# Pooled attention into a soft mixture of experts: carrying three row groups of the last expert, cutting fewer weights and tiles into halves, and moving the slot sums

## The chip, the cores and the metric

The kernel runs on one core of one Trainium2 chip. The metric is the device time of one execution in microseconds (us). The core has five engines that run their own instruction lists: PE (matrix products; its weight loads are shown apart as PEld), DVE and ACT (elementwise work), POOL (which here issues all loads but one) and SP (which issues the first load and all stores). Sixteen DMA engines move the data.

## The reference, cut to what matters

```python
# attention: q, k, v are (8, 8, 576, 64); keys and values are averaged over 8 tokens
k_p = k.reshape(B, H, Sp, 8, D).mean(axis=3)
v_p = v.reshape(B, H, Sp, 8, D).mean(axis=3)
attn = softmax(scale * q @ k_p.T)
x = (attn @ v_p) as (4608, 512)
# soft mixture: 8 experts, 4 slots each
logits = x @ phi                                  # (4608, 32)
d = softmax of logits over the 4608 tokens        # dispatch
slot_input = (d.T @ x).reshape(8, 4, 512)
h = maximum(slot_input[e] @ w1[e], 0)             # (4, 1024)
slot_out[e] = h @ w2[e]                           # (4, 512)
c = softmax of logits over the 32 slots           # combine
return c @ slot_out                               # (4608, 512) float32
```

w1 and w2 are 16.8 MB each in float32, the output is 9.4 MB.

## The kernel before, in words

**Attention and dispatch (up to about 124 us).** The batch is worked in four pairs. For each pair PE averages keys and values (`pool_stage`), turns keys and queries, makes scores (`score_unit`), and `u_tile` makes the attention's output next to its logits in `xsa`. `weigh` (L333) sums the logits over the heads on PE and takes the exponential on ACT into `ee`; `gather` (L341) multiplies `ee` with x on PE and collects the slot inputs; `turn` writes the transposed exponentials into `cT` (32 slots, repeated over four row groups of partitions, by tokens), with their sums over tokens in `C`. For the last pair this is written out in L475 to L513: tokens tiles 0 to 3, then 4 to 6, then 7 and 8.

**First layer (L525 to L545).** `hidden(i)` makes the hidden values of four experts at a time, four products beside one another in four column groups of the array; `turn_hidden(i)` turns them into `hT`. `recC` is the reciprocal of the dispatch sums.

**Second layer (L549).** `second_layer(e, j0, j1, half)` adds the row groups j0 to j1 (of eight, FJ) of `w2[e]` to `so_ps`, a PSUM tile with the slots' outputs; four row groups run beside one another on four column groups of the array. Weights come by DMA with a cast to bf16: experts 0 to 3 into `big`, 4 and 5 into `qTa`, the first three row groups of expert 6 into `xsa` (L473), all 512 columns wide. The last five row groups of expert 6 and all of expert 7 come in halves of 256 columns, first the left halves, then the right ones, each in the pieces of `PIECES` (L92, L498 to L506). All of these are issued by POOL in the order of the text.

**The order at the end.** From L516 on, the order on PE, ACT, DVE and SP is the order of the text: each engine takes its instructions as they are written, and waits where an operand isn't ready. POOL's order is that of the text throughout. The written-out list is L656 to L685. `busy(n)` (L581) is a float32 product into a tile that nobody reads, a filler for PE. `row_sums` (L405) sums the exponentials over the slots for all tokens, ten matmuls with one-hot weights that read `cT` with a step of half the rows of a store group; `turn_sums` (L414) turns and inverts them into `recR`.

**Carrying.** The output of a tile of 128 tokens is `c @ slot_out`. For the first CARRY = 4 tiles the last row group of expert 7 (J7 = FJ - 1) does not pass through the slots' sum: `hz` holds that group's hidden values times `recC` (L568), `zT` is `hz` times the tokens' exponentials (L571 to L575), and `product(n, cols, True)` adds `zT` times the weights (L615) to the tokens times `so_a` (L616), which is the slots' sum without that group, scaled by `recC` on ACT (L632). So `so_a` can be made before the last piece of weights is there. All other tiles use `so`, the scaled sum of everything (L639, L618).

**Output.** Tokens are split in store groups of 4, 4, 2, 4, 8 and 14 rows per partition, 128 tokens a row, 36 tiles in all (GROUPS, L57). `put` (L625) scales a tile by `recR` on ACT or DVE in turn; `store` (L607) is a DMA on SP. The first SPLIT = 10 tiles are made and stored by halves of the columns, two tiles a DMA; the rest with whole rows, a group a DMA.

```python
begin(half):  so_a <- so_ps (ACT);  products 0, 1 (carried);  second_layer(7, J7, FJ, half)
              products 2, 3 (carried);  put 0 (ACT), put 1 (DVE), store 0-1
              so <- so_ps (ACT);  put 2 (DVE), put 3 (ACT), store 2-3
```

Of the kernel before, what the change touches and what calls it, by code (L numbers as in the profile page):

```python
# [18 lines left out]
def kernel(  # L19
# [37 lines left out]
    for rows in (4, 4, 2, 4, 8, 14):  # L57
        GROUPS.append((rows, base))
        base += 128 * rows
# [81 lines left out]
    for _ in range(95):  # L141
        nc.tensor.matmul(out=first[0:32, 0:16], lhsT=zeros[:, 0:32], rhs=zeros[:, 0:16], start=True, stop=True)
# [6 lines left out]
    onehot = consts.tile([128, 2 * MAXC - 1], BF)  # L149
# [39 lines left out]
    hz = consts.tile([128, 128], BF)  # L189
    for i in range(4):  # L190
        nc.gpsimd.memset(hz[:, 32 * i:32 * i + 32], 0.0)
# [213 lines left out]
    def row_sums():  # L405

        ps = ps_m.tile([NC, 4, 128], FP, name="R_ps", tag="m")
        for c, (_, t) in enumerate(quads + rest):
            nc.tensor.matmul(out=ps[:, 0:2 * t.shape[1]].rearrange("p (s r) i -> p s r i", r=2),   # L409
                             lhsT=onehot[:, MAXC - 1 - c:MAXC - 1 - c + NC], rhs=t,  # L410
                             start=(c == 0), stop=(c == NC - 1), skip_group_check=True)
        nc.scalar.copy(out=sums, in_=ps)
# [60 lines left out]
    load_w2(xsa[:, 0:1], E - 2, 1, 0, CUT6)  # L473
# [16 lines left out]
    def half_home(e, half):  # L490
        if e == E - 1:
            flat = xsa[:, 1, half * FJ * HC:(half + 1) * FJ * HC]
        else:
            c0 = CUT6 * DM + half * (FJ - CUT6) * HC
            flat = xsa[:, 0, c0:c0 + (FJ - CUT6) * HC]
        return flat.rearrange("p (j c) -> p j c", c=HC)

    w2_half = {}  # L498
    for half, cols in enumerate(halves):
        for e, j0, j1 in PIECES:  # L500
            home = half_home(e, half)
            i = 0 if e == E - 1 else CUT6
            nc.gpsimd.dma_start(out=home[:, j0 - i:j1 - i],  # L503
                                in_=moe_w2[e].rearrange("(p j) d -> p j d", j=FJ)[:, j0:j1, cols])
            for j in range(j0, j1):
                w2_half[e, j, half] = home[:, j - i]  # L506
# [42 lines left out]
    def second_layer(e, j0=0, j1=FJ, half=None):  # L549
        cols = slice(0, DM) if half is None else halves[half]  # L550
        for fj in range(j0, j1):
            g = fj % NG
            nc.tensor.matmul(out=so_ps[g * NS:(g + 1) * NS, cols], lhsT=hT[:, e, fj],  # L553
                             rhs=w2_at[e, fj] if half is None else w2_half[e, fj, half],
# [5 lines left out]
    turn_hidden(1)  # L560
    nc.vector.reduce_sum(out=recC, in_=C, axis=AX.X)
# [4 lines left out]
    J7 = FJ - 1  # L566
    P7 = (E - 1) % NG * NS
    nc.vector.tensor_scalar(out=hz[P7:P7 + NS], in0=h_sb[(E - 1) // NG][P7:P7 + NS, J7:F:FJ], scalar1=recC[P7:P7 + NS],  # L568
                            scalar2=None, op0=ALU.mult)
# [13 lines left out]

    def tiny(count, n=128):
        for _ in range(count):
            nc.tensor.matmul(out=idle[:, 0:n], lhsT=cT[:, 0, 0:128], rhs=cT[:, 0, 0:n], start=True, stop=True)
# [13 lines left out]
    n = 0  # L600
# [10 lines left out]
    def product(n, cols, carried=False):  # L611
        ps = ps_f.tile([128, DM], FP, name="f_ps", tag="f")[:, 0:cols.stop - cols.start]
        if carried:
            half = halves.index(cols)
            nc.tensor.matmul(out=ps, lhsT=zT[:, n], rhs=w2_half[E - 1, J7, half], start=True, stop=False)  # L615
            nc.tensor.matmul(out=ps, lhsT=tokens(n), rhs=so_a[:, cols], start=False, stop=True)  # L616
        else:
            nc.tensor.matmul(out=ps, lhsT=tokens(n), rhs=so[:, cols], start=True, stop=True)  # L618
# [97 lines left out]
```

## Time and profile before

| what | value |
|---|---|
| median of three runs | 175.86 us (175.48 to 176.15) |
| profiled execution, its own time | 176.28 us |
| its span | 174.5 us |
| PE, DVE, ACT, POOL busy | 134.5, 92.8, 89.7, 18.6 us |
| moved by DMA, read from and written to HBM | 61.93 and 9.44 MB |
| first store issued, last store issued | 148.07, 162.5 us |

The span is what the profile covers; the execution's time is 1.78 us longer. A line of the timeline reads: start, time from first start to last end of the merged instructions, engine, line of the kernel, operation, output <- inputs, shapes, count, and in brackets how long the engine was idle before and what ended it. PEq, SPq and the like are an engine's instruction queue. A line of the view by stretches reads: the stretch in us, its length, busy time with the count of instructions for PE, PEld, DVE, ACT and POOL, the granted clock of PE (1.00 is full), the share of the 16 DMA engines, and GB/s. A line of DMA issues reads: output <- input, queue, operation, count, size, and us from issue to landing. Bytes are counted at the destination, so a load that casts from float32 to bf16 counts half of what it reads.

### The profile page before, as it was taken

What the parts mean: (1) busy time and instruction counts of PE and PEld (TensorE: products, weight loads), DVE (VectorE), ACT (ScalarE), POOL (GpSimd) and SP (SyncE); (2) the same over time, 40 slices, a digit from 0 to 9 for tenths busy, and PEclk for the clock granted to TensorE, in tenths of its full rate; (3) what the DMA queues carried; (4) which work ended last, traced back from release to release, by engine and by line L of the source; (5) the groups of instructions that cost most, each with busy time, mean ns of one, the idle gap of its engine ahead of it and who ended that gap; (6) DMA issues with size and microseconds to landing.
All of it is one profiled execution on the core that took longest, in us unless ns stands there. A gap on an engine that the chain in (4) does not pass through costs nothing.

```text
span 174.5 us, 3115 instructions
## 1 busy us (share of the span) xinstructions
PE 134.5 (77%) x1236; PEld 74.1 (42%) x1236; DVE 92.8 (53%) x255; ACT 89.7 (51%) x174; POOL 18.6 (11%) x38
## 2 busy tenths in 40 slices
PE   5005778999899999999999899477878999898000
PEld 5002253565455655556555445343443234443000
DVE  5403263478879568796688735831650001699200
ACT  3201338977787838969379854454021103899000
POOL 7100111022101040000010002206010020000000
PEclk9999999999999999999999858955899999999855
DMA  5999999999999999999999999999999999899994
GB/s 195 246 215 218 217 220 207 224 213 217 212 216 221 215 209 224 213 215 216 218 214 212 214 225 218 212 212 214 222 218 216 195 195 166 289 358 438 451 421 210
DMA packets 10558, 41.14 MB, mean 236 GB/s; under 512 B 673, under 2 KB 6561, under 8 KB 6833
## 3 DMA queue, kind: packets, MB, share of 16 engines
q0 software_dynamic: 7248, 30.48, 86.1%
q1 hardware_dynamic: 3296, 10.49, 15.4%
q8 instruction: 9, 0.15, 0.3%
q14 instruction: 5, 0.03, 0.0%
HBM read 61.93 MB, written 9.44 MB: 409 GB/s over the span
## 4 chain that ended last, share of the span: by engine, by line
PE 55%; ACT 19%; DVE 8%; DMA 7%; issue 3%; POOL 1%; DVEq 0%; ACTq 0%; POOLq 0%
PE pool_ps L232 10%; ACT exa L306 8%; PE G_ps L344 7%; DMA phi_f<-in_moe_phi_dram 7%; PE sc L304 6%; PE u_ps L319 5%; PE q_ps L264 5%; DVE w_sb L592 4%; PE idle_ps L582 3%; PE lg_ps L337 3%; PE so_ps L553 3%; PE R_ps L409 3%; ACT vmeans L238 2%; PE h_ps L532 2%; PE turn_ps L248 2%
## 5 line engine op out<-in xcount | busy, mean ns | idle before, releaser
L306 ACT ACTIVATE exa<-sc 72x576 bf16<-72x576 f32 x64 | 39.4, 652 | 5.0 <-PE sc L304 4.3
L330 DVE TENSOR_TENSOR xsa<-u_ps,rec 128x384 bf16<-128x384 f32 x66 | 35.8, 553 | 1.2
L319 PE MATMUL u_ps<-vp,exa 72*128 72x97 bf16 (+1 forms) x304 | 25.9, 214 | 2.2 <-DVE xsa L330 1.3
L319 PEld LDWEIGHTS <-exa 72*128 72x128 bf16 (+1 forms) x320 | 18.4, 103 | 14.5 <-issue 4.1
L304 PE MATMUL sc<-qTa,kp 64*72 64x288 bf16 x128 | 21.8, 307 | 1.8 <-ACT exa L306 1.3
L232 PE MATMUL pool_ps<-big,pmat 128*128 128x512 bf16 x64 | 18.6, 411 | 0.7 <-ACT qTa L268 0.6
L324 DVE RECIPROCAL rec<-u_ps 128x4 f32<-128x4 f32 x69 | 10.9, 172 | 12.9 <-PE u_ps L319 12.7
L344 PE MATMUL G_ps<-xsa,ee 128*128 128x512 bf16 x36 | 12.8, 504 | 1.7 <-ACT ee L338 1.7
L264 PE MATMUL q_ps<-ident,big 128*128 128x128 bf16 x144 | 11.6, 219 | 0.8 <-DVE qTa L270 0.3
L304 PEld LDWEIGHTS <-kp 64*72 64x72 bf16 x128 | 8.0, 108 | 8.2 <-issue 2.9
L618 PE MATMUL f_ps<-so,cT 128*128 128x512 bf16 (+1 forms) x38 | 9.8, 344 | 1.0 <-ACT w_sb L590 0.8
L240 DVE TENSOR_REDUCE rsum<-rest_ps 128x64 f32<-128x512 f32 x8 | 5.5, 691 | 9.3 <-PE rest_ps L236 9.1
L264 PEld LDWEIGHTS <-big 128*128 128x128 bf16 x144 | 8.7, 97 | 2.9 <-issue 1.2
L268 ACT COPY qTa<-q_ps 128x768 bf16<-128x768 bf16 x8 | 6.3, 794 | 7.0 <-PE q_ps L264 7.0
L592 DVE TENSOR_SCALAR w_sb<-f_ps,recR 128x512 f32<-128x512 f32 (+1 forms) x15 | 9.6, 706 | 0.5 <-PE f_ps L618 0.5
L270 DVE COPY qTa<-q_ps 128x768 bf16<-128x768 bf16 x16 | 8.7, 552 | 1.7 <-PE q_ps L264 1.6
L183 PE MATMUL phi_ps<-spread,sel 128*128 128x256 bf16 x4 | 1.3, 396 | 10.5 <-DVE spread L178 10.5
L590 ACT ACTIVATE w_sb<-f_ps,recR 128x512 f32<-128x512 f32 (+1 forms) x15 | 8.7, 660 | 0.5 <-PE f_ps L618 0.3
L503 POOL DMA_DIRECT2D xsa<-in_moe_w_dram x8 | 6.0, 748 | 26.8 <-DMA qTa<-in_moe_w_dram 9.6
L232 PEld LDWEIGHTS <-pmat 128*128 128x128 bf16 x64 | 5.8, 103 | 6.5 <-issue 2.1
L592 DVE TENSOR_SCALAR exa<-f_ps,recR 128x256 f32<-128x256 f32 x8 | 3.7, 481 | 8.8 <-PE f_ps L616 8.6
L337 PE MATMUL lg_ps<-xsa,ident 128*128 128x288 bf16 (+3 forms) x48 | 7.8, 286 | 0.3 <-ACT xsa L328 0.3
(107 smaller groups left out, 166.4 us busy)
## 6 DMA issues: line engine op xcount, KB each, us to landing
w_sb<-in_moe_w_dram POOLq DMA_DIRECT2D x2, 3072.0 KB, 37.4
big<-in_q_dram POOLq DMA_DIRECT2D x4, 1152.0 KB, 12.4
big<-in_v_dram POOLq DMA_DIRECT2D x4, 1152.0 KB, 16.1
big<-in_moe_w_dram POOLq DMA_DIRECT2D x1, 4096.0 KB, 40.2
out_dram<-w_sb SPq DMA_DIRECT2D x1, 3584.0 KB, 10.6
big<-in_k_dram POOLq DMA_DIRECT2D x3, 1152.0 KB, 22.0
w_sb<-in_moe_w_dram POOLq DMA_DIRECT2D x2, 1024.0 KB, 18.6
qTa<-in_moe_w_dram POOLq DMA_DIRECT2D x1, 2048.0 KB, 31.0
```

The source lines that it names most:

```text
L232: nc.tensor.matmul(out=ps, lhsT=pmat, rhs=src[:, t:full * POOL:POOL, :], start=(t == 0), stop=(t == POOL - 1))
L264: nc.tensor.transpose(out=ps[:, t].rearrange("p n i -> p (n i)"), in_=q_sb[pair][:, tt:tt + 2, :].rearrange("p t d -> p (t d)"), identity= ...
L270: nc.vector.tensor_copy(out=dst, in_=ps)
L304: nc.tensor.matmul(out=ps[:, r, 0:S // 2], lhsT=kp[pair][rows, n], rhs=qT[pair][rows, n].rearrange("p t i -> p (t i)"), start=True, stop=True)
L306: nc.scalar.activation(out=dst.rearrange("p r (i t) -> p r i t", t=NU), in_=ps[:, :, 0:S // 2].rearrange("p r (t i) -> p r i t", i=NI), fu ...
L319: nc.tensor.matmul(out=ps[rows, hh], lhsT=ex[b][:, hh].rearrange("p r t -> p (r t)")[:, c:c + rows.stop - rows.start], rhs=vp[(2 * pair + ...
L324: nc.vector.reciprocal(out=rec, in_=ps[:, :, XW])
L330: nc.vector.tensor_tensor(out=dst, in0=ps[:, :, 0:XW], in1=rec.rearrange("p h -> p h ()").to_broadcast([128, HQ, XW]), op=ALU.mult)
L337: nc.tensor.matmul(out=lg, lhsT=ident, rhs=x[:, t0:t1, h, D:XW], start=(h == 0), stop=(h == H - 1))
L344: nc.tensor.matmul(out=ps, lhsT=ee[:, t].rearrange("p g s -> p (g s)"), rhs=x[:, t, :, 0:D], start=(t == 0), stop=(t == 8))
L592: nc.vector.tensor_scalar(out=dst, in0=src, scalar1=by, scalar2=None, op0=ALU.mult)
L618: nc.tensor.matmul(out=ps, lhsT=tokens(n), rhs=so[:, cols], start=True, stop=True)
```

## The change

* **Store groups** become 4, 4, 4, 6, 10 and 8 rows; SPLIT goes from 10 to 8 tiles.
* **Weights**: expert 6 comes whole, in two DMAs of five and three row groups; only expert 7 (eight row groups) comes by halves, in pieces of 3, 2, 2 and 1 row groups.
* **Carrying**: three row groups of expert 7 instead of one. `hz` and `zT` get a dimension of three; `zT` is made by three products of 512 columns and three copies (`carried`), now behind the second layer of experts 0 to 3. In `begin`, tiles 0 and 1 first take the carried groups, then the slots' part, are scaled and stored; the rest of the second layer, tiles 2 and 3 (three carried products and one of the slots each) follow.
* **Slot sums**: `row_sums` runs right behind `turn_hidden(1)`, ahead of the second layer; its one-hot weights are 128 columns wide instead of 10.
* **The last pair's weighing** takes tokens tiles 4 to 8 in one step instead of two.
* **Fillers**: 512 columns; three times 512; 512; 512; 512 (before: 512, 512, 512, 256, 512, 256, 256). The start-up matmuls go from 95 to 85.

```diff
-    for rows in (4, 4, 2, 4, 8, 14):
+    for rows in (4, 4, 4, 6, 10, 8):
...
-    CUT6 = 3
+    J7 = FJ - 3
-    PIECES = ((E - 2, CUT6, FJ), (E - 1, 0, 4), (E - 1, 4, FJ - 1), (E - 1, FJ - 1, FJ))
+    PIECES = ((0, 3), (3, J7), (J7, FJ - 1), (FJ - 1, FJ))
...
-    for _ in range(95):
+    for _ in range(85):
...
-    hz = consts.tile([128, 128], BF)
+    hz = consts.tile([128, FJ - J7, 128], BF)
...
-                             lhsT=onehot[:, MAXC - 1 - c:MAXC - 1 - c + NC], rhs=t,
+                             lhsT=onehot[:, MAXC - 1 - c:MAXC - 1 - c + 128], rhs=t,
...
-    load_w2(xsa[:, 0:1], E - 2, 1, 0, CUT6)
+    load_w2(xsa[:, 0:1], E - 2, 1, 0, 5)
+    load_w2(xsa[:, 0:1], E - 2, 1, 5, FJ)
...
-    weigh(x, ee, 4, 7)
-    gather(x, G_ps, ee, 4, 7)
-    weigh(x, ee, 7, 9)
-    gather(x, G_ps, ee, 7, 9)
+    weigh(x, ee, 4, 9)
+    gather(x, G_ps, ee, 4, 9)
...
+        home = xsa[:, 1, half * FJ * HC:(half + 1) * FJ * HC].rearrange("p (j c) -> p j c", c=HC)
+        for j0, j1 in PIECES:
+            nc.gpsimd.dma_start(out=home[:, j0:j1], in_=moe_w2[E - 1].rearrange("(p j) d -> p j d", j=FJ)[:, j0:j1, cols])
...
     turn_hidden(1)
+    row_sums()
...
-    SPLIT, CARRY = 10, 4
-    z_ps = ps_f.tile([128, CARRY, 128], FP, name="z_ps", tag="f")
-    for s in range(CARRY // 2):
-        nc.tensor.matmul(out=z_ps[:, 2 * s:2 * s + 2], lhsT=hz, rhs=cT[:, :, s:s + 255:2], start=True, stop=True)
-    zT = post.tile([128, CARRY, 128], BF)
-    nc.scalar.copy(out=zT, in_=z_ps)
+    SPLIT, CARRY = 8, 4
+    zT = post.tile([128, FJ - J7, CARRY, 128], BF)
+    def carried():
+        for k in range(FJ - J7):
+            ps = ps_f.tile([128, CARRY, 128], FP, name="z_ps", tag="f")
+            nc.tensor.matmul(out=ps.rearrange("p (s r) i -> p s r i", r=2), lhsT=hz[:, k],
+                             rhs=cT[:, :, 0:64 * CARRY].rearrange("p r (i s) -> p s r i", s=CARRY // 2), start=True, stop=True)
+            if k % 2:
+                nc.vector.tensor_copy(out=zT[:, k], in_=ps)
+            else:
+                nc.scalar.copy(out=zT[:, k], in_=ps)
...
         scaled(0, so_a[:, cols], so_ps[:, cols], recC)
-        f = [product(n, cols, True) for n in range(2)]
-        second_layer(E - 1, J7, FJ, half)
-        f += [product(n, cols, True) for n in range(2, CARRY)]
+        f = [ps_f.tile([128, DM], FP, name="f_ps", tag="f")[:, 0:HC] for _ in range(CARRY)]
+        def from_z(n, j0, j1):
+            for j in range(j0, j1):
+                nc.tensor.matmul(out=f[n], lhsT=zT[:, j - J7, n], rhs=w2_half[j, half], start=(j == J7), stop=False)
+        def from_slots(n):
+            nc.tensor.matmul(out=f[n], lhsT=tokens(n), rhs=so_a[:, cols], start=False, stop=True)
+        for n in range(2):
+            from_z(n, J7, FJ - 1)
+        for n in range(2):
+            from_z(n, FJ - 1, FJ)
+        for n in range(2):
+            from_slots(n)
         put(0, cols, 0, f[0])
         put(1, cols, 1, f[1])
         store(0, 0, 2, cols)
+        second_layer(E - 1, J7, FJ, half)
+        for n in range(2, CARRY):
+            from_z(n, J7, FJ)
+            from_slots(n)
...
     for e in range(4):
         second_layer(e)
-    row_sums()
+    carried()
     busy(512)
     turn_sums()
-    busy(512)
-    busy(512)
+    for _ in range(3):
+        busy(512)
     for e in range(4, E - 2):
         second_layer(e)
-    busy(256)
-    second_layer(E - 2, 0, CUT6)
     busy(512)
-    for i, n in enumerate((256, 256, 0)):
-        second(PIECES[i:i + 1], 0)
-        if n:
-            busy(n)
+    second_layer(E - 2, 0, 5)
+    busy(512)
+    second_layer(E - 2, 5, FJ)
+    busy(512)
+    second_layer(E - 1, 0, 3, 0)
+    second_layer(E - 1, 3, J7, 0)
     begin(0)
     tiles(4, 6, 0)
+    second_layer(E - 1, 0, 3, 1)
     tiles(6, 8, 0)
-    second(PIECES[:2], 1)
-    tiles(8, 10, 0)
-    second(PIECES[2:-1], 1)
+    second_layer(E - 1, 3, J7, 1)
     begin(1)
-    for n in (4, 6, 8):
+    for n in (4, 6):
         tiles(n, n + 2, 1)
```

More of the change, by code (lines that the diff above doesn't have):

```diff
@@ L148 @@
     nc.vector.tensor_copy(out=identf, in_=ident[0:MAXC, 0:MAXC])
-    onehot = consts.tile([128, 2 * MAXC - 1], BF)
+    onehot = consts.tile([128, MAXC + 127], BF)
     nc.vector.memset(onehot, 0.0)
@@ L484 @@
     gather(x, G_ps, ee, 0, 4)
-    weigh(x, ee, 4, 7)
-    gather(x, G_ps, ee, 4, 7)
-    weigh(x, ee, 7, 9)
-    gather(x, G_ps, ee, 7, 9)
+    weigh(x, ee, 4, 9)
+    gather(x, G_ps, ee, 4, 9)
     add_up(NP - 1, G_ps, Gb)
[L490 to L496, printed above, removed]
     w2_half = {}
     for half, cols in enumerate(halves):
[L500 to L506, printed above, removed]
+        home = xsa[:, 1, half * FJ * HC:(half + 1) * FJ * HC].rearrange("p (j c) -> p j c", c=HC)
+        for j0, j1 in PIECES:
+            nc.gpsimd.dma_start(out=home[:, j0:j1], in_=moe_w2[E - 1].rearrange("(p j) d -> p j d", j=FJ)[:, j0:j1, cols])
+        for j in range(FJ):
+            w2_half[j, half] = home[:, j]
     si_ps = ps_u.tile([128, DJ, NS], BF, name="si_ps", tag="u")
@@ L609, in store, with product @@
         nc.sync.dma_start(out=dst[:, r0:r1, cols], in_=home[:, r0:r1, cols])
-    def product(n, cols, carried=False):
+    def product(n, cols):
         ps = ps_f.tile([128, DM], FP, name="f_ps", tag="f")[:, 0:cols.stop - cols.start]
[L613 to L618, printed above, removed]
+        nc.tensor.matmul(out=ps, lhsT=tokens(n), rhs=so[:, cols], start=True, stop=True)
         return ps
```

19 lines of the change are left out of this document (6 added, 13 removed).

## The prediction

> **What bounds the kernel now.** I began with the slices of the page, to see whether one resource runs through the whole span.
>
> ```profile
> span 174.5 us, 3115 instructions
> DMA  5999999999999999999999999999999999899994
> GB/s 195 246 215 218 217 220 207 224 213 217 212 216 221 215 209 224 213 215 216 218 214 212 214 225 218 212 212 214 222 218 216 195 195 166 289 358 438 451 421 210
> ```
>
> The DMA engines are full in every slice but the last: loads at about 215 GB/s up to slice 30, a slower stretch, then stores. So the kernel is a load stream followed by a store stream, and time can be won only where the two streams run slowly or where they meet. I looked at those places with the view by stretches, then with the timeline.
>
> ```profile
> 139.00:147.00 8.00, 7.64 (x50) 3.07 (x50) 0.40 (x2) 0.47 (x1) 1.35 (x2) 1.00 1.42 194
> 150.00:156.00 6.00, 5.30 (x28) 2.42 (x26) 4.67 (x10) 5.57 (x13) 0.00 (x0) 1.00 1.03 341
> 157.00:159.00 2.00, 1.80 (x8) 0.69 (x7) 2.00 (x4) 1.92 (x4) 0.00 (x0) 1.00 1.02 418
> ```
>
> ```profile
> 147.50:148.00 0.50, 0.50 (x5) 0.36 (x5) 0.48 (x1) 0.50 (x2) 0.00 (x0) 1.00 0.83 110
> 148.50:149.00 0.50, 0.45 (x8) 0.07 (x6) 0.48 (x3) 0.50 (x2) 0.00 (x0) 1.00 0.12 22
> 149.00:149.50 0.50, 0.50 (x11) 0.29 (x11) 0.42 (x2) 0.50 (x2) 0.00 (x0) 1.00 0.99 323
> ```
>
> The last column is GB/s. The load stream dries up from 147.5, the store stream starts at 149.0: a hole of 1.3 us or so. Half-width stores then flow at 341 GB/s, whole rows at 418. From 149.0 the stream has no second hole, so **the end of the span hangs on the first store's issue** and on the length of the store stream.
>
> ```profile
> 146.12 0.29 PE L553 MATMUL so_ps<-xsa,hT 128*32 128x256 bf16 x3
> 146.45 0.47 ACT L590 ACTIVATE so_a<-so_ps,recC 128x256 bf16<-128x256 f32 x1 [7.76 <-PE so_ps L553]
> 146.98 0.27 PE L616 MATMUL f_ps<-so_a,cT 128*128 128x256 bf16 x1 [0.36 <-ACT so_a L590]
> 148.07 2.15 SPq L609 DMA_DIRECT2D out_dram<-exa  x4
> 150.22 0.47 ACT L590 ACTIVATE so_a<-so_ps,recC 128x256 bf16<-128x256 f32 x1
> 151.82 2.15 SPq L609 DMA_DIRECT2D out_dram<-exa  x4
> ```
>
> The first store is issued at 148.07 and its data flow 0.93 us later. What came before it: PE, ACT's scaling, PE again. Was PE waiting for weights? The time of issue on POOL plus the time to landing tells.
>
> ```profile
> 107.82 0.70 POOL L113 DMA_DIRECT2D qTa<-in_moe_w_dram  x1 [18.74 <-ACT cT L364]
> 108.51 0.57 POOL L113 DMA_DIRECT2D xsa<-in_moe_w_dram  x1
> 129.09 0.77 POOL L503 DMA_DIRECT2D xsa<-in_moe_w_dram  x1 [8.12 <-DMA big<-in_moe_w_dram]
> 139.41 0.76 POOL L503 DMA_DIRECT2D xsa<-in_moe_w_dram  x1 [9.55 <-DMA qTa<-in_moe_w_dram]
> 141.30 0.59 POOL L503 DMA_DIRECT2D xsa<-in_moe_w_dram  x1 [1.12 <-DMA xsa<-in_moe_w_dram]
> ```
>
> ```profile
> 119.51 0.59 POOL L503 DMA_DIRECT2D xsa<-in_moe_w_dram  x1
> ```
>
> ```profile
> qTa<-in_moe_w_dram POOLq DMA_DIRECT2D x1, 2048.0 KB, 31.0
> xsa<-in_moe_w_dram POOLq DMA_DIRECT2D x1, 384.0 KB, 32.2
> ```
>
> ```profile
> xsa<-in_moe_w_dram POOLq DMA_DIRECT2D x1, 64.0 KB, 25.6
> ```
>
> ```profile
> xsa<-in_moe_w_dram POOLq DMA_DIRECT2D x1, 64.0 KB, 8.2
> ```
>
> Experts 4 and 5 land at 107.82 + 31.0 = 138.8, the first three row groups of expert 6 at 108.51 + 32.2 = 140.7, the last piece of the first half at 119.51 + 25.6 = 145.1, the last piece of all at 141.30 + 8.2 = 149.5. PE uses the 145.1 piece only behind the row of 146.12, over a microsecond late. In this execution the first store is paced by PE's own list, fillers and slot sums included, and not by the weights.
>
> **The change, part by part.** *When weights land.* The bytes stay the same, only order and width change. Between 140.7 and 149.5 there are 26 half-width row groups of 64 KB: 8.8 / 26 = 0.338 us each. The 384 KB of whole rows took 140.7 - 138.8 = 1.9 us, 0.316 us per 64 KB. Afterwards all of expert 6 comes in whole rows: 16 x 0.316 = 5.06 us, so its five groups land at 142.0 and its last three at 143.9. The first half of expert 7 is 8 x 0.338 = 2.7 us, in pieces of 3, 2, 2 and 1 groups that land at 144.9, 145.6, 146.2 and **146.6**; the second half ends at 149.3. So the load stream is 0.2 us shorter, but the piece on which the first store depends comes 1.5 us later than today, because the first half no longer stops at a half of expert 6. POOL issues one DMA more. The rows at 129.09, 139.41 and 141.30 show it waiting for the eighth DMA before each; the last issue will wait for 143.9 and fall at about 144.4, 4.9 us ahead of its landing where today it has 8.2. I cost it at nothing, since seven DMAs are queued ahead of it; if that cover is gone the last piece lands up to 1 us later, for which only the second half waits.
>
> *PE's list.*
>
> ```profile
> 128.41 1.49 PE L544 MATMUL hT_ps<-ident,h_sb 128*128 128x128 bf16 x16
> 131.74 1.91 PE L553 MATMUL so_ps<-big,hT 128*32 128x512 bf16 x32
> 133.48 4.60 PE L409 MATMUL R_ps<-cT,onehot 128*10 128x512 bf16 x10
> 134.59 0.10 PEld L409 LDWEIGHTS <-onehot 128*10 128x10 bf16 x1 [0.34 <-issue]
> 135.04 0.11 PEld L409 LDWEIGHTS <-onehot 128*10 128x10 bf16 x1 [0.34 <-issue]
> 135.83 0.11 PEld L409 LDWEIGHTS <-onehot 128*10 128x10 bf16 x1 [0.68 <-issue]
> 139.41 1.98 PE L582 MATMUL idle_ps<-cT 128*128 128x512 f32 x4
> ```
>
> The slot sums go into the gap between 129.9 and 131.7, where PE waits for DVE's copies. Their matmuls read tokens with a step of half the rows of a group: from one weight load to the next 0.45 us for the eight-row group (step 4), 0.79 for the 14-row group (step 7), 0.113 per unit of step. With groups of 4, 4, 4, 6, 10, 8: 3 x 0.23 + 0.34 + 2 x 0.56 + 2 x 0.45 + 0.45 for the two half-size ones = 3.5 us against 4.6. No row shows steps 3 and 5, nor the 128-column one-hot weights; the bounds are 2.3 (ten at step 2) and 4.6 (as now), and I stay at 3.5, the line through the two rows. They end at 133.4. The first four experts take 1.74 (133.48 - 131.74): 135.1. The three carried products, 512 columns at step 2, 0.7: 135.8; their weights come from DVE while the slot sums run, and their copies on ACT and DVE lie beside the fillers. A 512-column filler is two of the four records in 1.98 us, 1.0: 136.8; the four transposes 0.4; three fillers 2.8 : 140.0; experts 4 and 5 take 1.0; a filler: 142.0. From here the weights decide: five groups (landed 142.0) 0.5, a filler 1.0, three groups at 143.9, done by 144.3, a filler to 145.3, three half groups, then two more that landed at 145.6, done 145.9. ACT's scaling of 0.47 then ends by 146.5 and **is hidden** behind the last two pieces (146.2 and 146.6): that is what carrying three groups buys. Two products of the last carried group (0.22 us), and the slot product starts at 146.85. From there to the store it was 148.07 - 146.98 = 1.09; the second slot product now follows directly, 0.1 less. First store: **147.85, 0.2 earlier than 148.07**. Bounds: 147.5 if pieces land at the 0.316 pace and nothing waits, 148.4 if the PE list is half a microsecond longer than worked out.
>
> ```profile
> 118.11 1.03 ACT L328 ACTIVATE xsa<-sc,rec 128x96 bf16<-128x96 f32 x4 [0.82 <-DVE rec L324]
> 118.43 0.85 PE L337 MATMUL lg_ps<-xsa,ident 128*128 128x96 bf16 x8
> 122.22 1.04 PE L344 MATMUL G_ps<-xsa,ee 128*128 128x512 bf16 x2 [0.47 <-ACT ee L338]
> ```
>
> The joined weighing of tokens 4 to 8 must wait for ACT's last tile (119.14): eight logit matmuls of 160 columns instead of 96 (1.25), one exponential (an estimate of 0.7), five gathers at 0.43 (2.3 with the last one's depth) end at 123.5 instead of 123.26. That is +0.25 us on PE, between 0 and 0.5, covered by the 0.4 us that PE waits for 143.9. The larger clears on POOL and DVE lie in the first microseconds and ten fewer start-up matmuls ahead of a DMA wait: nothing.
>
> *The store stream.* Two tiles, 524 KB, move from 341 to 418 GB/s: 1.54 - 1.25 = **-0.28 us**. A page's specification speaks against this term: the Trainium skill, "DMA: Bandwidth & Descriptors", section Specifications, asks 512 bytes for line rate, which half rows of 1 KB fulfil, so by it the term is zero and the sum 0.28 us higher. This trace disagrees, 341 against 418 GB/s.
>
> *The seam between the halves.* Today five half stores (1.31 MB, 3.85 us at 341 GB/s) bridge the 3.75 us from 148.07 to 151.82. Afterwards four, 3.08 us, must do. On ACT one tile's scaling goes (about 0.4); but tiles 2 and 3 now take four products each instead of two, 4 x 0.11 later, of which ACT sees a part. I take 3.45 us, bounds 3.2 and 3.75: a new hole of **+0.35 us** (0.1 to 0.7). The next seam, where whole rows begin, comes out even.
>
> Sum: -0.2 - 0.28 + 0.35 = **-0.1 us**. The profiled execution took 176.28 us, its span and 1.78 us around it, 0.4 above the median of the three runs, 175.86 us; I put the difference on the median: **175.8 us**. What a measurement of this kernel can tell from no change is about 0.5%, 0.9 us.
>
> **Rivals.**
>
> *PE still paces the first store* (the change does not do what it says: the carried groups wait for ACT as now). If sums at steps 3 and 5 or the fillers cost more than the 0.4 us of slack, the first store goes to 148.4 and the time to 176.3. For it: all of PE's slack is one short wait. Chance 0.17.
>
> *The hole closes.* The landing rows lag the stream: flow drops at 147.5, the last landing is 149.5. If the lag shrinks with fewer 512-byte pieces, the first half lands up to a microsecond earlier, PE's list allowing 147.5 or less, and the seam stays shut: -0.6 to -1.6, about 174.8. Against: the lag has stood through the whole half-width stretch. Chance 0.18.
>
> *The clock does not come back.*
>
> ```profile
> 116.50:119.90 3.40, 2.82 (x17) 1.51 (x18) 0.81 (x4) 2.31 (x9) 1.91 (x3) 0.50 1.03 217
> 119.90:123.30 3.40, 2.92 (x16) 1.39 (x17) 0.00 (x1) 0.38 (x1) 1.07 (x2) 0.50 1.01 212
> 123.30:126.70 3.40, 3.02 (x50) 1.68 (x52) 2.94 (x7) 0.00 (x0) 0.00 (x0) 1.00 1.08 226
> ```
>
> PE (first pair) was busy 2.82 of 3.40 us and stayed at a granted 0.50; after 2.92 it got 1.00. The joined weighing leaves PE idle longer just there. If its busy time falls to 2.8, the next stretch runs at half speed: 1.7 us lost, 0.3 covered: 177.3, slower. The Trainium skill, "TensorE: Matmul & The Clock Gate", the table "Why this matters for your kernels", ties a fall to idle gaps of over about 3 us; by that rule nothing happens here, but the trace shows half clock with no such gap. Against the rival: the matmuls are the same, only shifted by 0.25 us. Chance 0.12.
>
> *The seam opens wide*: 3.75 + 0.45 us with a bridge of 3.08 is a hole of 1.1, and with a first store that is no earlier 176.7 to 177.0. It decides once ACT waits for all four added products. Chance 0.08.
>
> **How the numbers follow.** Forecast 0.45 (175.2 to 176.3 its own range), PE-paced 0.17, hole closed 0.18, clock 0.12, wide seam 0.08. Both first cases lie within 0.5% (0.62); faster 0.18; slower 0.20. Leaving about a tenth on each side: 174.8 to 177.1.
>
> **What would show it.** In the changed profile: expert 6's last landing near 143.9 and the first half's near 146.6; PE waiting for DMA ahead of them where it waits for none now; ACT's first scaling ended before the last carried product; the first store's issue near 147.85; a dip in GB/s near 151.8; half stores until 155 and whole rows at 418 behind. A first store more than 0.5 us from 147.85, or a granted clock of 0.50 after 123.3, makes the prediction wrong.

## The result: slower by 0.44%, and the profile after

The changed kernel takes 176.37 us (median of 11, 176.23 to 177.01), the kernel before 175.53 in the same session (median of 11, lowest 175.38): a ratio of 1.0044, 95% interval 1.0029 to 1.0058. The time lies in the forecast's range and, by the bound of 0.5%, counts as no change; but the forecast of -0.1 us had the wrong sign and the loss is measurable. The ratios leave out a few longer executions, which came up in the kernel before (one of these eleven, 181.75 us) and in some of its variants, and never in the changed kernel or its variants. The profiled execution took 176.51 us.

The page of the kernel after, its span, its row of GB/s and the shares of the chain that ended last:

```profile
span 174.7 us, 3099 instructions
GB/s 195 241 217 220 217 217 215 217 215 217 210 220 216 215 218 217 211 222 212 216 214 218 221 214 214 212 221 219 216 212 212 215 195 146 297 364 443 425 451 184
PE 40%; DMA 24%; ACT 19%; DVE 5%; issue 3%; POOL 1%; DVEq 0%; ACTq 0%; POOLq 0%
```

The slower stretch between loads and stores is still there (195, 146). The chain of waits around the first store, from 143 us on, begins with these steps, each with start, length and what:

```profile
115.23 30.90 DMA xsa<-in_moe_w_dram
146.13 0.04 issue
146.17 0.81 PE f_ps L624 x6
```

Now a load releases PE: the chain goes straight from the piece of expert 7 issued at 115.23 to the carried products at 146.17. The timeline of the kernel after around that point:

```profile
143.79 0.40 PE L542 MATMUL so_ps<-xsa,hT 128*32 128x512 bf16 x3 [0.20 <-DMA xsa<-in_moe_w_dram]
145.75 0.47 ACT L582 ACTIVATE so_a<-so_ps,recC 128x256 bf16<-128x256 f32 x1 [11.24 <-PE so_ps L542]
146.17 0.81 PE L624 MATMUL f_ps<-xsa,zT 128*128 128x256 bf16 x6 [0.46 <-DMA xsa<-in_moe_w_dram]
146.82 0.38 PE L627 MATMUL f_ps<-so_a,cT 128*128 128x256 bf16 x2
147.81 3.64 SPq L601 DMA_DIRECT2D out_dram<-exa  x5
148.00 1.58 DVE L584 TENSOR_SCALAR exa<-f_ps,recR 128x256 f32<-128x256 f32 x3 [0.28 <-PE f_ps L627]
148.44 1.24 ACT L582 ACTIVATE exa<-f_ps,recR 128x256 f32<-128x256 f32 x3 [0.47 <-PE f_ps L627]
```

Expert 6 is there at 143.8, `so_a` is scaled ahead of need, PE waits 0.46 us for weights and the first store goes out at 147.81. Then comes something new: ACT's scaling of tile 3 waits for four more products until 148.44, so that the second store follows at 148.94, 1.13 us after the first. The view by stretches shows what that costs (last column GB/s):

```profile
148.50:149.00 0.50, 0.50 (x7) 0.21 (x5) 0.45 (x1) 0.50 (x2) 0.00 (x0) 1.00 0.58 186
149.00:149.50 0.50, 0.50 (x6) 0.27 (x5) 0.44 (x2) 0.50 (x2) 0.00 (x0) 1.00 0.97 330
149.50:150.00 0.50, 0.50 (x6) 0.43 (x5) 0.08 (x1) 0.50 (x2) 0.00 (x0) 1.00 0.33 113
150.00:150.50 0.50, 0.50 (x7) 0.19 (x4) 0.00 (x0) 0.14 (x2) 0.00 (x0) 1.00 1.05 344
...
152.50:153.00 0.50, 0.50 (x4) 0.25 (x3) 0.33 (x2) 0.50 (x3) 0.00 (x0) 1.00 0.82 268
153.00:153.50 0.50, 0.47 (x3) 0.10 (x1) 0.50 (x1) 0.50 (x2) 0.00 (x0) 1.00 0.77 266
```

One store of two half tiles flows for some 0.75 us, the next one comes 1.13 later: a gap of about 0.35 us at 149.5 to 150. Another 0.2 are missing at 152.5 to 153.5, behind the first store of the second half, where the second one (152.21) again follows 1.14 after the first (151.07).

### The profile page after: what moved, and what is told of

It is laid out like the page before. It is cut to its first block, busy times and chain, and to the rows that moved or that the text cites. A ratio compares the mean times of both kernels' runs of the same rounds, so it can differ in the third digit from the quotient of the medians.

```text
span 174.7 us, 3099 instructions
## 1 busy us (share of the span) xinstructions
PE 134.5 (77%) x1228; PEld 75.1 (43%) x1228; DVE 94.0 (54%) x255; ACT 89.2 (51%) x173; POOL 18.9 (11%) x39
## 4 chain that ended last, share of the span: by engine, by line
PE 40%; DMA 24%; ACT 19%; DVE 5%; issue 3%; POOL 1%; DVEq 0%; ACTq 0%; POOLq 0%
DMA xsa<-in_moe_w_dram 18%; PE pool_ps L232 9%; ACT exa L306 8%; DMA phi_f<-in_moe_phi_dram 7%; PE sc L304 6%; PE u_ps L319 5%; PE q_ps L264 5%; PE G_ps L344 4%; ACT vmeans L238 2%; PE f_ps L605 2%; PE lg_ps L337 2%; PE f_ps L624 2%; PE turn_ps L248 2%; DVE w_sb L584 2%; ACT cT L364 1%
## 5 line engine op out<-in xcount | busy, mean ns | idle before, releaser
L232 PE MATMUL pool_ps<-big,pmat 128*128 128x512 bf16 x64 | 18.1, 403 | 0.7 <-ACT qTa L268 0.6
L344 PE MATMUL G_ps<-xsa,ee 128*128 128x512 bf16 x36 | 10.7, 441 | 1.5 <-ACT ee L338 1.5
L584 DVE TENSOR_SCALAR w_sb<-f_ps,recR 128x512 f32<-128x512 f32 x14 | 9.3, 743 | 0.2 <-PE f_ps L605 0.2
L493 POOL DMA_DIRECT2D xsa<-in_moe_w_dram x8 | 5.5, 690 | 33.3 <-DMA big<-in_moe_w_dram 12.6
L582 ACT ACTIVATE w_sb<-f_ps,recR 128x512 f32<-128x512 f32 x14 | 8.3, 703 | 0.1
L238 ACT CAST vmeans<-pool_ps 128x1024 bf16<-128x1024 f32 x4 | 4.0, 1012 | 6.8 <-PE pool_ps L232 6.8
```

The lines of the kernel that those rows point to most:

```text
L232: nc.tensor.matmul(out=ps, lhsT=pmat, rhs=src[:, t:full * POOL:POOL, :], start=(t == 0), stop=(t == POOL - 1))
L344: nc.tensor.matmul(out=ps, lhsT=ee[:, t].rearrange("p g s -> p (g s)"), rhs=x[:, t, :, 0:D], start=(t == 0), stop=(t == 8))
L582: nc.scalar.activation(out=dst, in_=src, func=AF.Copy, scale=by)
L584: nc.vector.tensor_scalar(out=dst, in0=src, scalar1=by, scalar2=None, op0=ALU.mult)
```

## The experiments

The theory of the load order, L in the quotes, says that the first half's last landing, 1.5 us later, costs the time; against it stood the new gap behind the first store, the slot sums, and the way the before side is measured.

**The kernel before, profiled again** (b_again, b_again2, b_again3; no edit).

> The kernel before, unchanged, profiled once more. Theory L (the first store is held by a landing in the changed kernel, by PE's list only in some executions of the kernel before): if this execution's time is near 175.5 us, PE reaches the first layer at about 121 us instead of 124.8 and the first store is issued before 147.6, not at 148.07. Rival S (only the seams between stores count): the first store is issued near 148.07 whatever the time is.

> The kernel before, unchanged, profiled a third time, to meet an execution of its faster group. Theory P: if its time is below 175.7 us, the turning of the hidden values starts before 127.4 us instead of 128.4 and the first store is issued at 146.7 to 147.4; if it is near 176.2 us, both are as in the first profile (128.4 and 148.06). Rival: the first store at 148.06 in a fast execution as well.

> The kernel before, unchanged, profiled a fourth time, for the same question. Theory P: time and first store go together, 175.4 to 175.6 us with 146.7 to 147.4, 176.2 with 148.06. Rival: they do not.

The three executions took 176.27, 175.45 and 175.73 us. Their first stores, the last two by their timelines, b_again2 and then b_again3:

```profile
124.39 1.48 PE L544 MATMUL hT_ps<-ident,h_sb 128*128 128x128 bf16 x16
145.06 0.47 ACT L590 ACTIVATE so_a<-so_ps,recC 128x256 bf16<-128x256 f32 x1 [8.11 <-PE so_ps L553]
146.67 2.15 SPq L609 DMA_DIRECT2D out_dram<-exa  x4
```

```profile
124.29 1.47 PE L544 MATMUL hT_ps<-ident,h_sb 128*128 128x128 bf16 x16
147.44 2.16 SPq L609 DMA_DIRECT2D out_dram<-exa  x4
```

b_again repeats the execution that the prediction was made from: the turning at 128.40, the first store at 148.06. So the kernel before has no one time of arrival: PE turns the hidden values anywhere from 124.3 to 128.4, and the first store goes out between 146.67 and 148.07. Over all sessions 63 of its 122 executions took 175.16 to 175.65 us; the one that I had was one of the others. Only b_again2 is a profile from that group; that the rest of it has an early first store too is inferred from the times. Two stretches of b_again, then of b_again2, show the difference (behind the five busy times the granted clock):

```profile
120.00:124.00 4.00, 3.69 (x28) 1.87 (x32) 2.26 (x6) 0.07 (x1) 0.00 (x0) 0.50 1.02 215
124.00:128.00 4.00, 4.00 (x52) 1.66 (x48) 1.03 (x2) 0.60 (x1) 0.00 (x0) 0.64 1.03 215
```

```profile
120.00:124.00 4.00, 3.95 (x69) 2.14 (x73) 2.58 (x7) 0.60 (x1) 0.00 (x0) 1.00 0.98 207
124.00:128.00 4.00, 2.21 (x30) 1.36 (x19) 2.28 (x6) 0.78 (x2) 0.00 (x0) 1.00 1.06 221
```

Where half clock falls on the first layer, PE arrives 4 us later with the same list. b_again3 turned as early as b_again2, but had half clock from 127.9 to 134.7, and its first store came 0.77 later.

An early first store is not worth its whole length. In b_again2 the store stream runs dry between the halves, as it does not in b_again:

```profile
151.50:152.00 0.50, 0.45 (x4) 0.23 (x3) 0.48 (x3) 0.50 (x2) 0.00 (x0) 1.00 0.24 82
```

The last weights land near 149.5 in both, and the second half's first store goes out at 151.04 and 151.81: the first store is 1.39 us earlier, the span 0.8 shorter (173.7 and 174.5). So the prediction's "the end of the span hangs on the first store's issue" holds only as far as the stream behind it has no hole.

**The load order alone, and undone** (b_new_loads, a_old_loads).

```diff
 b_new_loads, on the kernel before (second list likewise)
     load_w2(xsa[:, 0:1], E - 2, 1, 0, CUT6)
+    load_w2(xsa[:, 0:1], E - 2, 1, CUT6, FJ)
-    PIECES = ((E - 2, CUT6, FJ), (E - 1, 0, 4), (E - 1, 4, FJ - 1), (E - 1, FJ - 1, FJ))
+    PIECES = ((E - 1, 0, 4), (E - 1, 4, FJ - 1), (E - 1, FJ - 1, FJ))
+    second_layer(E - 2, CUT6, FJ)
```

```diff
 a_old_loads, on the kernel after: expert 6's row groups 3 to 7 by halves again
-    load_w2(xsa[:, 0:1], E - 2, 1, 0, 5)
-    load_w2(xsa[:, 0:1], E - 2, 1, 5, FJ)
+    load_w2(xsa[:, 0:1], E - 2, 1, 0, 3)
+        nc.gpsimd.dma_start(out=home6, in_=moe_w2[E - 2].rearrange("(p j) d -> p j d", j=FJ)[:, 3:FJ, cols])
```

> The kernel before with one part of the change alone: expert 6 comes whole, so that the first half of expert 7 ends at 146.6 instead of 145.1. One row group is carried, ten tiles by halves, slot sums where they were. Theory L: the first store is issued at 147.9 to 148.2 in every execution; 0.4 to 0.8 us slower than the kernel before (ratio 1.002 to 1.005), most of what the whole change costs. Rival S: no change, 0.998 to 1.001, since the seams are as before.

> The changed kernel with the order of loads as before (the last five row groups of expert 6 by halves), all else as changed. Theory L (the changed kernel's first store waits for a piece that lands 1.5 us later than before): first store at 146.3 to 146.8 instead of 147.81; 0.3 to 0.8 us faster than the changed kernel (ratio to the kernel before 1.000 to 1.002), not the full 1.2, since four half stores then leave a hole of about 0.6 us ahead of the second half, whose last piece lands at 149.5. Rival (the seams alone cost): the hole moves from one seam to the next and the time stays, ratio 1.004.

The new order on the kernel before: 176.6 us (176.2 at the lowest), ratio 1.0061 (1.0043 to 1.0080). It costs as much as the whole change, and no execution lies below 176.2. Its profile (176.51 us) has no gap in the stores, only a late first one:

```profile
144.11 0.60 PE L554 MATMUL so_ps<-xsa,hT 128*32 128x512 bf16 x5
146.51 0.47 ACT L591 ACTIVATE so_a<-so_ps,recC 128x256 bf16<-128x256 f32 x1 [8.02 <-PE so_ps L554]
148.12 2.15 SPq L610 DMA_DIRECT2D out_dram<-exa  x4
```

PE was late in this execution too (it turned the hidden values at 128.21), and no wait for a load shows there. But the last piece that `so_a` needs landed at 146.13, and PE took it up at 146.17, 0.34 ahead of the scaling: an earlier PE could have won some 0.04 us at that place.

The old order under the rest of the change: 175.87 (175.73 to 176.27), ratio 1.0009 (0.9991 to 1.0027), 0.5 us less than the change as it was made. Its first store went out at 146.59, but the second again 1.13 later, and with the early start four half stores no longer reach the second half's landing. Its stretches, with two nearly empty ones:

```profile
151.00:151.50 0.50, 0.50 (x7) 0.46 (x5) 0.32 (x1) 0.14 (x1) 0.00 (x0) 1.00 0.11 37
151.50:152.00 0.50, 0.50 (x5) 0.31 (x4) 0.44 (x2) 0.38 (x2) 0.00 (x0) 1.00 0.27 96
```

So 1.2 us of earlier store (147.81 to 146.59) became 0.5 us of time. Theory L holds, and the seams are the second cause.

**How many groups are carried, and in which order** (a_carry1, a_mid).

```diff
 a_carry1, on the kernel after
-    J7 = FJ - 3
+    J7 = FJ - 1
-    PIECES = ((0, 3), (3, J7), (J7, FJ - 1), (FJ - 1, FJ))
+    PIECES = ((0, 3), (3, 5), (5, 7), (7, 8))
```

```diff
 a_mid, on the kernel after, in begin
-        second_layer(E - 1, J7, FJ, half)
         for n in range(2, CARRY):
             from_z(n, J7, FJ)
             from_slots(n)
-        scaled(0, so[:, cols], so_ps[:, cols], recC)
+        second_layer(E - 1, J7, FJ, half)
         put(2, cols, 1, f[2])
         put(3, cols, 0, f[3])
         store(0, 2, 4, cols)
+        scaled(0, so[:, cols], so_ps[:, cols], recC)
```

> The changed kernel with one carried row group instead of three, everything else as changed. Tiles 2 and 3 take two products each again. Theory S: the second store follows the first by about 0.7 us instead of 1.13, the hole at 149.5 closes, the first store is issued about 0.1 later (147.9); 0.2 to 0.4 us faster than the changed kernel (ratio to the kernel before 1.002 to 1.003). Theory L: the end hangs on the first store alone, so 0.0 to 0.1 us slower than the changed kernel (1.004 to 1.006). If carrying three groups does what it is for, the first store is issued 0.3 us or more later.

> The changed kernel with the products of tiles 2 and 3 ahead of the rest of the second layer, and their scaling ahead of that of the slots' sum. The first store stays at 147.8, the second is issued at about 148.65 instead of 148.94. Theory S (the hole at 149.5 behind the first store is worth its length): 0.2 to 0.3 us faster than the changed kernel, ratio to the kernel before 1.002 to 1.003. Theory L (only the first store counts): 1.004 as the changed kernel.

One carried group takes 176.02 (175.75 to 176.44), ratio 1.0022 (1.0008 to 1.0036), 0.35 us less than three. In its profile (176.19 us) expert 6 is used at 144.19, the first store follows 4.21 later at 148.40, where three carried groups have 147.81 - 143.79 = 4.02: in this pair of profiles they buy **0.19 us**. But its second store comes 0.69 after the first, and the stream has no gap:

```profile
149.50:150.00 0.50, 0.50 (x7) 0.28 (x7) 0.45 (x1) 0.43 (x3) 0.00 (x0) 1.00 1.01 330
150.00:150.50 0.50, 0.12 (x2) 0.03 (x1) 0.00 (x0) 0.41 (x2) 0.00 (x0) 1.00 1.03 334
```

Making tiles 2 and 3 ahead of the rest of the second layer was meant to close the gap. It took 177.27 (177.11 to 177.72), ratio 1.0098 (1.0080 to 1.0116): a miss. In its profile (177.72 us) the second store came 0.81 after the first, but the third 1.30 after that, since `so` now waits behind them; the gap moved and more followed:

```profile
150.50:151.00 0.50, 0.50 (x7) 0.43 (x6) 0.30 (x1) 0.50 (x2) 0.00 (x0) 1.00 0.53 180
151.00:151.50 0.50, 0.50 (x6) 0.35 (x4) 0.00 (x0) 0.26 (x1) 0.00 (x0) 1.00 0.43 150
```

**Fewer half tiles** (a_old_groups: ten half tiles and the old store groups on the kernel after).

```diff
-    for rows in (4, 4, 4, 6, 10, 8):
+    for rows in (4, 4, 2, 4, 8, 14):
-    SPLIT, CARRY = 8, 4
+    SPLIT, CARRY = 10, 4
-    for n in (4, 6):
+    for n in (4, 6, 8):
```

> The changed kernel with the store groups and the ten tiles by halves of the kernel before. The slot sums take 4.6 us again, covered by the microsecond that PE waits for experts 4 and 5. First store unchanged at 147.8, five half stores bridge to the second half, so the later dip near 153 goes (0.2 us), but 0.24 us more for the half rows: ratio within 0.001 of the changed kernel, 1.003 to 1.005. If whole rows at 418 GB/s are worth the 0.28 us of the forecast and the seams nothing, 1.006.

176.32 (176.02 to 177.29), ratio 1.0044 (1.0021 to 1.0068): as the kernel after. The 0.28 us that two tiles should win does not arrive. Where it goes is seen only in part: the dip at 152.5 to 153.5 is absent here, and in the one profile the first store goes out later (148.08), since the half's last piece landed 0.3 later than in the profile of the kernel after.

**The work taken off PE** (b_sums_early, b_less_fill, on the kernel before).

```diff
 b_sums_early
     turn_hidden(1)
+    row_sums()
...
     for e in range(4):
         second_layer(e)
-    row_sums()
```

```diff
 b_less_fill
-    busy(512)
-    for i, n in enumerate((256, 256, 0)):
+    for i, n in enumerate((0, 0, 0)):
```

> The kernel before with one part of the change alone: the slot sums behind the turning of the hidden values, all fillers kept, so that PE's list is about 1.5 us shorter and the clock stays granted. Theory P (in the profiled execution of the kernel before PE was late by about a microsecond, in most of its executions it is not, or less so): the profile shows the first store at 146.7 to 147.0 instead of 148.07, no hole between the halves since five stores bridge it, and an execution of the profiled kind near 175.2; the median falls by 0.2 to 0.5 us (ratio 0.997 to 0.999) and the spread upwards to 176.2 goes. Rival (PE is late by the same 1.3 us in every execution): the median falls by 1.0 to 1.3 us (ratio 0.993 to 0.994).

> The kernel before without the 512-column filler and the two 256-column fillers ahead of the last weights of the first half (2.3 us less on PE). Theory L: PE then waits for weights in every execution, the first store is issued at 146.4 to 147.0, the hole between loads and stores shrinks, and the time falls by 0.3 to 0.8 us below the kernel before (ratio 0.996 to 0.998), with a smaller spread. Rival S: the first store earlier, but a hole opens between the halves, because the second half's weights land at 149.5 all the same: ratio 1.000.

The slot sums moved alone: 175.65 (175.42 to 176.62), ratio 1.0020 (0.9997 to 1.0042), no gain. The first store of its profile went out at 146.98, as expected, but the spread stayed: five of twelve executions took 176.47 to 176.62. The waits of PE from its profile (line, releaser, total, times, longest), and its stretches:

```profile
PE so_ps L553 <- DMA qTa<-in_moe_w_dram: 2.9, 1, 2.9
```

```profile
135.00:138.50 3.50, 0.96 (x3) 0.22 (x2) 0.00 (x0) 0.00 (x0) 0.00 (x0) 0.99 1.01 202
138.50:142.00 3.50, 3.14 (x21) 1.10 (x20) 0.00 (x0) 0.00 (x0) 1.35 (x2) 0.52 1.36 194
```

What PE saves it waits for experts 4 and 5, and behind a stretch with 0.96 of 3.50 us busy the next one ran at 0.52. Without the last fillers the spread grows to 175.29 to 179.03, and the ratio is 1.0025 (0.9982 to 1.0068): the expected gain was missed. In its profile:

```profile
142.50:146.00 3.50, 1.57 (x16) 0.62 (x16) 0.00 (x0) 0.58 (x2) 0.00 (x0) 1.00 1.45 196
146.00:149.50 3.50, 3.50 (x24) 1.56 (x23) 1.99 (x5) 2.21 (x5) 0.00 (x0) 0.51 1.10 230
```

Its first store went out at 146.67 as in the best execution of before, but the clock was halved there, and the second store came 1.2 later. So the time that the fillers take on PE is no loss; that they win any is not shown.

**Two and three parts undone** (a_two_undone: old load order, one carried group; a_three_undone: the old store groups as well; the edits are those shown). What stays of the change: early slot sums, 128-column one-hot weights, joined weighing, fillers, order of the products.

> The changed kernel with three parts undone: the order of loads, the store groups with ten tiles by halves, and the carrying of three row groups (one again). What stays of the change: slot sums ahead of the second layer with 128-column one-hot weights, the joined weighing, the fillers, and the new order of products. Theory L plus S (a landing holds the first store, and the seams cost their length): first store at 146.6 to 147.0, no hole behind it and none between the halves; 174.8 to 175.2 us, faster than both kernels (ratio to the kernel before 0.995 to 0.998) and without a second group of executions a microsecond above. Rival (the fastest executions of the kernel before are already at a floor near 175.4 that the order of work does not move): 0.999 to 1.001.

> The changed kernel with the order of loads and the carrying of one row group as before, but with the new store groups and eight tiles by halves: against the kernel with three parts undone it sizes the seam between the halves. Theory S: first store at 146.6 to 147.0, four half stores (3.1 us) do not reach to the second half, whose first store cannot leave before 150.6 because its last piece lands near 149.3; a hole of 0.5 to 0.9 us near 151, less 0.24 us for fewer half rows: 175.3 to 175.7 us, 0.2 to 0.6 us slower than with three parts undone (ratio to the kernel before 0.998 to 1.001). Rival (the seam is hidden, whole rows count): 174.9, 0.2 faster than with three parts undone.

Three undone: **175.12** (175.04 to 175.63), ratio 0.9962 (0.9937 to 0.9987), faster than both kernels. Two undone: 175.80 (175.63 to 176.27), ratio 1.0010 (0.9992 to 1.0028), a little above the expected 175.3 to 175.7. With an early first store (146.76) the four half stores do not bridge to the second half, ten half tiles do but for one short dip. Stretches of a_two_undone, then the one dip of a_three_undone:

```profile
151.00:151.50 0.50, 0.44 (x5) 0.24 (x3) 0.45 (x2) 0.47 (x2) 0.00 (x0) 1.00 0.09 33
151.50:152.00 0.50, 0.50 (x5) 0.34 (x4) 0.43 (x2) 0.50 (x2) 0.00 (x0) 1.00 0.07 25
```

```profile
151.50:152.00 0.50, 0.50 (x5) 0.25 (x3) 0.46 (x2) 0.50 (x2) 0.00 (x0) 1.00 0.26 90
```

**The end of the span** (b_pool_16, b_pool_1). a_three_undone and b_again2 issue their first stores at 146.65 and 146.67, and their last land at 161.68 + 10.6 = 172.28 and 161.74 + 10.5 = 172.24; yet the spans end at 173.3 and 173.7. The trace has POOL's own list pausing there: up to 172.8 both lists run alike, but the next instruction, which clears semaphores, starts at 173.2 in b_again2 (first line) and at 172.8 in a_three_undone:

```profile
L711 POOLq EVENT_SEMAPHORE_RANGE_CLEAR  x1: 139/139/139, 173.2 to 173.2; - x1
L715 POOLq EVENT_SEMAPHORE_RANGE_CLEAR  x1: 139/139/139, 172.8 to 172.8; - x1
```

The DMA view of 172 to 176 of b_again2 has one packet of eight kilobytes, here with its place in forty slices (173.9, behind the end of the span):

```profile
GB/s 0 0 0 0 0 0 0 0 0 0 0 0 0 0 0 0 0 0 0 82 0 0 0 0 0 0 0 0 0 0 0 0 0 0 0 0 0 0 0 0
q14 instruction: 1, 0.01, 0.5%
```

In a_three_undone that stretch is empty, and the packet comes at 146 to 148. Its place goes with the number of POOL's instructions on the page: behind the last store with 37 and 38 (before and its variants), at 152 to 154 with 39 (after), at 146 to 148 with 40. So I took it for a piece of POOL's instruction list; no view names the engine that a packet is for.

```diff
 on the kernel before, behind POOL's last load (b_pool_1: one clear)
+    pad = consts.tile([128, 16], BF)
+    for i in range(16):
+        nc.gpsimd.memset(pad[:, i:i + 1], 0.0)
```

> The kernel before with 16 one-column clears on POOL, of a tile that nobody reads, behind POOL's last issue of a load. Nothing that the stores wait for changes. Theory P: all kernels with 37 or 38 POOL instructions in the page (before and its variants) fetch an 8 KB piece of instructions some 1 us behind the last store's data, and end 1.4 us behind the last store's landing; all with 39 or 40 fetch it at 146 to 152 and end 1.0 us behind the landing. So POOL's list crosses into a new piece of code in its closing part. Sixteen more instructions move the crossing ahead of the end: the fetch comes before 160, the span ends 1.0 us behind the landing, and the time is 0.4 us shorter in each of the executions: ratio 0.9970 to 0.9985, lowest 175.0. Rival Q: the 0.4 us comes from something else in the changed kernel (fewer PE instructions, 128-column one-hot weights); then the time stays, ratio 0.999 to 1.001.

> As the run with 16 clears, with only one. Theory P: it goes either way by where the border lies. If the fetch still comes behind the last store, the time is that of before (ratio 0.999 to 1.001); if one instruction is enough, it is 0.4 us shorter, as with 16. In both cases the place of the fetch and the distance from the last landing to the end of the span (1.4 or 1.0 us) go together. Rival Q: they do not go together.

With 16 clears the packet came at 144 to 146, and the span of the profiled execution (174.8) ended 1.0 us behind the last landing (163.16 + 10.6 = 173.8). The lowest four of twelve executions took 174.97 to 175.14, where the lowest ten of before took 175.38 to 175.49: 0.4 shorter, as theory P has it. But six of the twelve took 176.47 to 176.60, and the ratio is 1.0004 (0.9977 to 1.0032): the expected ratio was missed. Its profile (176.60 us) is one of those six, and its stretches show why:

```profile
124.00:128.00 4.00, 1.74 (x18) 1.27 (x19) 1.95 (x5) 1.18 (x2) 0.00 (x0) 0.93 1.04 217
128.00:132.00 4.00, 3.45 (x33) 1.46 (x33) 0.00 (x0) 0.00 (x0) 0.77 (x1) 0.50 1.06 223
132.00:136.00 4.00, 4.00 (x12) 0.87 (x8) 0.00 (x0) 0.00 (x0) 0.00 (x0) 0.71 0.98 207
```

PE turned early (123.92), then was busy 1.74 of 4 us waiting for DVE's `hz` and for the weights of experts 0 to 3, and got a clock of 0.50 and 0.71 for the next eight: first store 148.71. That hole in PE's work is the one that the moved slot sums fill. With one clear the packet still came behind the last store (profiled execution 182.57 us), and the ratio was 1.0025 (1.0002 to 1.0047; lowest 175.53): no gain, as P allows. POOL then has 39 instructions on the page, as in the kernel after, where the packet comes early: the number alone does not fix the place.

## Why the prediction was wrong

*What held.* Expert 6's last three groups at 143.8 (143.9 forecast), the piece that PE waits for at 146.1 (146.2), the half's last piece at 146.4 (146.6), `so_a` hidden by carrying, the first store at 147.81 (147.85). The second half's first store (151.07) followed the first half's by 3.26 us, forecast at 3.45 with bounds of 3.2 and 3.75. The slot sums took 3.67 us for 3.5; from start to start, step 3 took 0.33 us and step 5 0.55, on the forecast's line. The joined weighing cost nothing: its logit matmuls began before ACT's last tile was done, and from that tile's end (115.57) to the last gather's (119.24) 3.67 us passed, for 4.12 before (119.14 to 123.26). Their rows in the kernel after:

```profile
114.86 1.27 PE L337 MATMUL lg_ps<-xsa,ident 128*128 128x160 bf16 x8
116.93 2.31 PE L344 MATMUL G_ps<-xsa,ee 128*128 128x512 bf16 x5 [0.80 <-ACT ee L338]
127.55 3.67 PE L409 MATMUL R_ps<-cT,onehot 128*128 128x512 bf16 x10
```

*The step that failed* is "In this execution the first store is paced by PE's own list", carried over by "I put the difference on the median". It was true of the execution, not of the median. An execution near the median of before (b_again2) has PE earlier and the first store at 146.67, because the first half lands by 145.1. The change moves that landing to 146.4, and in its profile the first store goes out at 147.81; no execution of the changed kernel took less than 176.23. So the first store comes not 0.2 us earlier, but 1.14 later than in b_again2. Against b_again2 the account closes, on the profiled executions and with the trace's times to a hundredth: first store +1.14, from there to the last landing +0.25 (25.83 for 25.58), from the last landing to the end of the span -0.29 (1.11 for 1.40): +1.1, the difference of the spans, 174.75 and 173.65. Of the 1.06 us between the two executions' times, 0.82 lie already between b_again and b_again2. Against b_again, of the kind that the forecast was made from, the change is still 0.24 us slower where -0.1 was forecast, and that is the next term.

*The second failed term* is the seam's +0.35. I looked for it between the halves, near 151.8, where the stream of the kernel after has no hole (328 GB/s at 151.5 to 152). The extra carried products delay ACT behind the **first** store, by the very wait that I named for tiles 2 and 3. From first store to last landing the profiled executions took 25.84 us after and 25.04 before, +0.8 where -0.28 + 0.35 were forecast. The gaps at 149.5 and 153 are 0.6 of the 25.84; a_carry1, without them, takes 24.91. Beside the 25.04 of before, with ten half tiles and no gap, that leaves 0.13 for the whole rows where 0.28 was forecast. The last 0.3 lie in the final transfer (landed 11.4 us after its issue, 11.0 in a_carry1) and stay open.

*A term that I did not have*: 0.3 to 0.4 us at the end. They go with the place of the last 8 KB fetch, a gain of the change by accident, and they are also what a_three_undone wins over the best execution of before: both have the same first store and the same last landing. Over the other executions of before it wins by its narrow spread.

*The rivals.* "PE still paces" did not happen, and "the hole closes" neither. "The seam opens wide" named the right cause, ACT waiting for the added products, at the wrong seam. The clock rival came about in half: this execution of after had half clock up to 124.5, past the 123.3 that the prediction named as a sign of being wrong, and still PE waited for weights at the end, so it did not hold the first store:

```profile
116.50:119.90 3.40, 2.90 (x10) 1.20 (x10) 0.62 (x2) 0.37 (x1) 0.00 (x1) 0.50 1.06 222
119.90:123.30 3.40, 3.29 (x33) 1.60 (x37) 1.99 (x7) 0.00 (x0) 0.00 (x0) 0.50 0.98 205
124.50:128.00 3.50, 3.44 (x54) 1.94 (x43) 1.63 (x3) 1.19 (x2) 0.00 (x0) 1.00 1.05 218
```

The Trainium skill, "DMA: Bandwidth & Descriptors", section Specifications, by which half rows cost nothing, came out right on the time of a_old_groups but not on the rate: half rows still flow at 330 to 350 GB/s, and what took the gain is seen only in part.

Two readings of the prediction are off without bearing on its sum: the DMA engines are half empty in the first slice as well as in the last, and three fillers of 1.0 us were put at 2.8.

## What to carry to other kernels

Profile the base kernel two or three times before a term of one execution goes onto the median: the engine that is late in one may be early in most, and a change that moves a landing then costs what the early ones had. Where a load stream meets a store stream, ask when the last bytes land that the first store needs, and whether each further store is issued within the transfer of the one before it: an earlier first store is worth only what no later hole takes back (here 0.8 of 1.39 us). Work taken off an engine ahead of a wait is no gain until the wait goes, and may cost it its clock.

## What the runs showed of the hardware

* Half clock came behind stretches in which PE was busy 0.96 of 3.50 us (b_sums_early), 1.57 of 3.50 (b_less_fill) and 1.74 of 4.00 (b_pool_16), none with a single pause above 2.9 us. It also stood at 0.50 through 116.5 to 123.3 of the kernel after with 2.90 and 3.29 of 3.40 busy. The rule behind it was not tried separately.
* The trace has instructions coming by DMA, in packets of 8 KB on queue 14 and of 16 KB on queue 8. One packet of queue 14 behind the last store went with an end that is 0.3 to 0.4 us longer (1.4 against 1.0 to 1.1 us from the last landing to the end of the span) and a pause of 0.4 us in POOL's list; 16 clears of no use on POOL took the late packet and the longer end away. That the packet is POOL's and that the pause is for it are inferred.
* A matmul of 512 bf16 columns that reads them with a step took, at full clock and from its start to the next one's, 0.23 us at step 2, 0.33 at step 3, 0.45 at step 4, 0.55 at step 5 and 0.79 at step 7 (slot sums, steps 3 and 5 in the kernel after, 7 in the kernel before).
